# Gated attention and two mixture layers on one core: results of a unit stored one turn later, small units transposed in their first layer's arm, five banks for the first layer

## The chip, the cores and the metric

The program runs on one core of a Trainium2 chip. The metric is the device time of one execution in microseconds (us). The kernel before has a median of 763.64 us over three runs (763.48 to 764.53).

## What is computed

Three stages: a gated linear attention, a dense layer with the maximum of three products, and a mixture of eight experts in which each of 3072 tokens goes to the one expert with the largest logit. The change touches the third only.

```python
def _moe2_ref(x, w_gate, w_output_gate, w1, w2):
    ...
    e_idx = np.argmax(logits, axis=1)
    ...
    for e in range(E):                      # 8 experts
        mask = e_idx == e
        h = np.maximum(x[mask] @ w1[e], 0.0)          # 384 -> 1024
        ye = h @ w2[e]                                # 1024 -> 384
        out[mask] = gate_w[mask, None] * eom[mask, e, None] * ye
```

## The kernel before

**Units.** The tokens of each expert are cut into units of at most 256 tokens; the last unit of an expert may carry a tail of up to 64 more. Which unit belongs to which expert, and how full it is, is found on the chip, so the code of each unit has arms that registers choose (`by_kind`, L896 to L902, and `tc.If`). The kinds are 0 (256 tokens, two tiles of 128), 1 (64 or fewer, "alone"), 2 (256 and a tail of 64: three tiles) and 3 (128 or fewer: one tile). With these inputs fifteen units run. Units 0 and 1 are interleaved with the end of the dense layer. Units 2 to 14 have a turn each, `turn(u)` (from L1278), of kinds 0, 0, 2, **1**, 2, 0, 0, 0, 2, **1, 1**, 2, 3; turns 10 and later stand nested under a guard (L1298), and turns 15 to 19 are jumped over.

**A turn**, in program order on all engines: `load_meta(u+2)`; `gather(u+2)`, three indirect DMAs by POOL that fetch token rows `xg`; the low half of the split of w2 (cast on ACT L644, rest on DVE L645); `up(u)`, the first layer; the high half of the split; the weight DMA of s1 for u+2 by SP (L847); `tx(u+1)`, which transposes the next unit's rows into `cx` (L880, L887, L888) or, for kind 1, into `xF` (L891); `split1(u+1)`, the split of the next unit's w1 (six casts on ACT, six subtractions on DVE); `down(u)`, the second layer; and the weight DMA of s2. Each engine follows its own queue in this order and meets the others only through semaphores. PE's clock is granted in the profile's rows as a share of full speed.

**First layer** (`up_some`, L918): eight slices f of the hidden width, nine matmuls each, into one of three PSUM banks of pool psM in rotation. ACT (L919) and DVE (L922) take a bank away before PE may fill it again. For kind 1 (`alone` in `up`), the weights move and the 64 tokens stand still: twelve matmuls of 512 columns (L909) into one bank, copied by ACT as a whole into `hF` (L932).

**Second layer** (`down_tile`, L961 and L966): per tile 24 matmuls, then ACT scales by the gate into a tile `yo` (L973). For kind 1 (`alone` in `down`), PE first transposes `hF` (L985), ACT (L990) and DVE (L988) take the rectified halves, then sixteen matmuls of 384 columns follow (L909) and a sum of two halves (L948, L949, L950).

**Results.** `yo` comes from seven rotating tiles, and its scatter to `out` is issued by POOL inside the arm (`put`, L938), as soon as the tile is written. POOL therefore reads the kind and branches as PE, ACT and DVE do.

## Time and profile before

| | us |
|---|---|
| median of 3 runs | 763.64 |
| the profiled execution | 759.59 |
| its span, first to last instruction | 757.8 |
| PE busy | 705.9 (93%) |
| ACT busy / DVE busy / POOL busy | 288.5 / 397.7 / 126.8 |
| mean granted clock of TensorE | 0.978 |
| last matmul ends | 738.1 |

The profile counts an engine as busy while an instruction of it executes. Idle time of an engine is put down to the event that came last before it went on (its releaser). [...] The stretch that the change touches begins with the first layer of unit 0, at about 445 us.

### The profile page before, as it was taken

The page shows a single profiled execution, that of the slowest core. Times are in us where ns is not written, and L with a number is a line of the kernel's source. Part 1 is how long each engine was busy: PE and PEld are TensorE (multiplying, and loading weights), DVE is VectorE, ACT ScalarE, POOL GpSimd, SP SyncE. Part 2 cuts the span into 40 slices and gives each one's busy share as a digit, 9 for nine tenths or more (in the row PEclk, how much of TensorE's full clock was granted, in tenths as well). Part 3 has the DMA queues.
Part 4 walks back from the last instruction along what each step waited for, and adds up shares of the span by engine and source line. Part 5 has one row for each costly group of instructions (what it writes and reads, how often), then busy time and mean ns, then how long its engine had stood idle before and what let it go on. Part 6 is the DMA issues. An engine that isn't in the chain of part 4 may idle for free. (4 is left out here: it accounts for less than half of the span.)

```text
span 757.8 us, 14282 instructions
## 1 busy us (share of the span) xinstructions
PE 705.9 (93%) x5056; PEld 656.3 (87%) x5056; DVE 397.7 (52%) x929; ACT 288.5 (38%) x752; POOL 126.8 (17%) x136
## 2 busy tenths in 40 slices
PE   8999999999899999999999999999989999977980
PEld 8989999798799999999999999999949899954970
DVE  7968976477957547364143566532237422213640
ACT  4455344454444424335131243332236423224540
POOL 1000000011121202111111130422232322231220
PEclk9999999999999999999999999999989999997995
DMA  9823400651412215000000060214553113666310
GB/s 265 340 57 137 144 1 22 181 134 45 124 51 73 69 40 131 15 24 5 22 19 10 22 229 22 62 58 138 208 214 112 52 51 132 204 237 218 99 43 17
DMA packets 23407, 76.33 MB, mean 101 GB/s; under 512 B 8026, under 2 KB 12132, under 8 KB 20208
## 3 DMA queue, kind: packets, MB, share of 16 engines
q1 hardware_dynamic: 17424, 60.95, 24.6%
q0 software_dynamic: 4704, 12.91, 5.4%
q8 instruction: 67, 1.10, 0.6%
q10 hardware_dynamic: 1152, 0.89, 0.4%
q14 instruction: 60, 0.49, 0.2%
HBM read 89.26 MB, written 9.94 MB: 131 GB/s over the span
## 5 line engine op out<-in xcount | busy, mean ns | idle before, releaser
L918 PE MATMUL psM<-cx,w1H 128*128 128x256 f32 (+1 forms) x576 | 112.1, 292 | 5.3 <-DVE ch L922 4.9
L482 POOL TENSOR_TENSOR hL<-hm,hH 128x384 fp32r<-128x384 f32 x36 | 42.2, 1172 | 396.6 <-ACT hH L477 396.6
L456 PE MATMUL hps<-xH,wH 128*128 128x384 f32 x432 | 103.9, 347 | 1.4 <-ACT xH L367 1.3
L456 PE MATMUL hps<-xH,wL 128*128 128x384 f32 x432 | 98.4, 335 | 1.6 <-DVE wL L425 1.6
L918 PEld LDWEIGHTS psM<-cx,w1H 128*128 128x128 f32 x576 | 91.3, 188 | 8.8 <-DVE ch L922 4.3
L456 PE MATMUL hps<-xL,wH 128*128 128x384 f32 x432 | 98.6, 335 | 0.0
L961 PE MATMUL psP<-w2H,ch 128*128 128x384 f32 x368 | 96.8, 338 | 1.1 <-ACT w2H L644 1.1
L922 DVE SCALAR_TENSOR_TENSOR ch<-psM,ch 128x256 fp32r<-128x256 f32 (+1 forms) x128 | 43.9, 371 | 95.2 <-ACT ch L919 92.1
L918 PE MATMUL psM<-cx,w1L 128*128 128x256 f32 (+1 forms) x288 | 83.6, 290 | 0.0
L456 PEld LDWEIGHTS hps<-xH,wH 128*128 128x128 f32 x432 | 74.1, 188 | 7.4 <-ACT xH L367 2.1
L456 PEld LDWEIGHTS hps<-xH,wL 128*128 128x128 f32 x432 | 76.9, 188 | 2.3 <-DVE wL L425 2.3
L456 PEld LDWEIGHTS hps<-xL,wH 128*128 128x128 f32 x432 | 77.3, 188 | 0.2 <-DVE xL L368 0.2
L492 PE MATMUL ops<-wo,hH 128*128 128x400 f32 x258 | 68.5, 346 | 0.2
L961 PEld LDWEIGHTS psP<-w2H,ch 128*128 128x128 f32 x368 | 66.6, 188 | 2.0 <-issue 1.3
L463 DVE TENSOR_TENSOR hm<-hm,hps 128x384 f32<-128x384 f32 x48 | 26.4, 551 | 69.7 <-PE hps L456 62.7
L919 ACT ACTIVATE ch<-psM 128x256 fp32r<-128x256 f32 (+1 forms) x96 | 37.7, 402 | 64.8 <-PE psM L918 55.4
L938 POOL DMA_INDIRECT out<-yo,sidx x30 | 31.1, 1038 | 185.8 <-ACT yo L973 147.8
L961 PE MATMUL psP<-w2L,ch 128*128 128x384 f32 x184 | 61.5, 334 | 0.0
L857 POOL DMA_INDIRECT xg<-x2d,gidx x49 | 50.4, 1029 | 30.1 <-PE psM L918 12.2
L918 PEld LDWEIGHTS psM<-cx,w1L 128*128 128x128 f32 x288 | 54.2, 188 | 0.0
L477 ACT CAST hH<-hm 128x384 fp32r<-128x384 f32 x43 | 22.0, 513 | 81.0 <-DVE hm L466 77.2
L492 PEld LDWEIGHTS ops<-wo,hH 128*128 128x128 f32 x258 | 47.0, 188 | 1.3 <-ACT hH L477 0.5
(238 smaller groups left out, 1111.5 us busy)
## 6 DMA issues: line engine op xcount, KB each, us to landing
s1a<-in_ew SPq DMA_DIRECT2D x9, 1536.0 KB
s2a<-in_ew SPq DMA_DIRECT2D x9, 1536.0 KB
s1b<-in_ew SPq DMA_DIRECT2D x7, 1536.0 KB
s2b<-in_ew SPq DMA_DIRECT2D x7, 1536.0 KB
ws<-in_w SPq DMA_DIRECT2D x6, 1152.0 KB
at<-in_al SPq DMA_DIRECT2D x16, 336.9 KB
vt<-in_v SPq DMA_DIRECT2D x8, 576.0 KB
x2d<-xs SPq DMA_DIRECT2D x24, 192.0 KB
```

The costliest lines, as they stand in the source:

```text
L456: mm(ps, slab(a, f)[:, w, k], b[i][:, k], start=(n == 0), stop=(n == 8))
L463: nc.vector.tensor_max(m, m, ps)
L477: nc.scalar.copy(hH[i, f], m)
L482: (nc.gpsimd if not general and i > 1 else nc.vector).tensor_sub(hL[i, f], hps["m"], hH[i, f].bitcast(F32))
L492: mm(ps[:, :DM + NG], a[i, f][:, ts_], wo[f // 3][:, b, f % 3], start=(f + n == 0), stop=(f + n == 7))
L857: nc.gpsimd.indirect_dma_start(out=xg[u % 2, t][:p], out_offset=None, in_=x2d[:n, :], in_offset=bass.IndirectOffsetOnAxis(ap=gidx[:p, 3 * ...
L918: mm(ps, w[:, k, f * 128:(f + 1) * 128], x[:, k, :n], start=(k + m == 0), stop=(k + m == 4))
L919: nc.scalar.activation(chid(0, f, slice(0, n)), ps, AF.Relu)
L922: nc.vector.scalar_tensor_tensor(C["h"][f // 4][:, f % 4, to:to + b - a], ps[:, a:b], 0.0, chid(0, f, slice(a, b)).bitcast(F32), op0=ALU.m ...
L938: nc.gpsimd.indirect_dma_start(out=out[:, :], out_offset=bass.IndirectOffsetOnAxis(ap=sidx[:p, c:c + 1], axis=0), in_=y[:p], in_offset=Non ...
L961: mm(ps[:, :DM], chid(x, f, slice(128 * t, 128 * t + 128)), w[:, f], start=(f + n == 0), stop=(f == NE - 1 and n == 2))
```

## The change

1. **Results.** Three fixed tiles `C["y"]`, set to zero by POOL at the start, take the results of every unit. `put(u-1, ...)` stands in turn u behind `gather(u+2)`, outside all arms: three scatters each turn (two for the first units), whatever the kind; rows that carry no token have an index that the scatter leaves out. The last unit's three scatters come after all turns, with indices that DVE copied to `C["at"]`. POOL no longer reads the kind and has no arms.
2. **Small units.** In kind 1 the first layer goes in two halves of 256 columns (two banks, two copies), and the transposes of `hF` with their rectification move from `down`'s arm to the end of `up`'s arm, ahead of `tx(u+1)` and `split1(u+1)`.
3. **Banks.** In `up_some`, slices 3 and 4 use the two banks of pool psH: five banks in turn instead of three.
4. **Arms.** In `down`, tile 0 of kinds 0, 2 and 3 is one piece of code; the kind is asked after it.

```diff
@@ load_meta
-        kind[u] = nc.values_load(..., engines=(ET.PE, ET.Activation, ET.DVE, ET.Pool),
+        kind[u] = nc.values_load(..., engines=(ET.PE, ET.Activation, ET.DVE),
@@ hidden
+        C["y"] = [bp.tile([128, DM], F32, tag="hL", name="yo", bufs=7) for _ in range(3)]
+        for y in C["y"]:
+            nc.gpsimd.memset(y, 0.0)
@@ up_some
-            ps = bank(psM, "M", "psM1")[:, :n]
+            ps = (bank(C["psH"], "H", "psH") if f in (3, 4) else bank(psM, "M", "psM1"))[:, :n]
@@ up: alone
-            ps = bank(psM, "M", "psM1")
-            w = C["s1"][u % 2]
-            for k in range(3):
-                x = C["xF"][:, k * 128:k * 128 + 64]
-                halves(ps, 512, (x, x), [w[:, k, g * 512:(g + 1) * 512] for g in range(2)], k == 0, k == 2)
-            nc.scalar.copy(C["hF"][:, :512], ps)
+            w, h = C["s1"][u % 2], C["hF"]
+            for a in range(0, 512, 256):
+                ps = bank(psM, "M", "psM1")
+                for k in range(3):
+                    x = C["xF"][:, k * 128:k * 128 + 64]
+                    halves(ps, 256, (x, x), [w[:, k, g * 512 + a:g * 512 + a + 256] for g in range(2)], k == 0, k == 2)
+                nc.scalar.copy(h[:, a:a + 256], ps[:, :256])
+            for a in range(0, 512, 256):
+                ps = bank(C["psH"], "H", "psH")
+                for f in range(2):
+                    nc.tensor.transpose(ps[:, f * 128:(f + 1) * 128], h[:, a + f * 128:a + (f + 1) * 128], ident)
+                hs = h[:, 512 + a:768 + a]
+                if a:
+                    nc.vector.tensor_scalar_max(hs, ps[:, :256], 0.0)
+                else:
+                    nc.scalar.activation(hs, ps[:, :256], AF.Relu)
@@ put
+    def scatter(t, at):
+        p = WIDTH[t]
+        nc.gpsimd.indirect_dma_start(out=out[:, :], out_offset=bass.IndirectOffsetOnAxis(ap=at[:p], axis=0),
+                                     in_=C["y"][t][:p], in_offset=None, bounds_check=NTOK - 1, oob_is_err=False)
+    def put(u, tiles=3):
+        for t in range(tiles):
+            scatter(t, sidx[:, 3 * u + t:3 * u + t + 1])
@@ put_sum, down_tile
-        y, lo = out_tile(), bp.tile([128, DM], F32, tag="hm", name="ylo")
+        y, lo = C["y"][t], bp.tile([128, DM], F32, tag="hm", name="ylo")
...
-        put(u, t, y, 64)
...
+        nc.scalar.activation(C["y"][t], ps[:, :DM], AF.Copy, scale=gate[u % 2][:, t:t + 1])
@@ down
-            h = C["hF"]
-            for g in range(2):
-                p = bank(C["psH"], "H", "psH")
-                for f in range(2):
-                    fs = slice((2 * g + f) * 128, (2 * g + f + 1) * 128)
-                    nc.tensor.transpose(p[:, f * 128:(f + 1) * 128], h[:, fs], ident)
...
-        by_kind(u, {1: alone, 2: tiles(3), 3: tiles(1)}, tiles(2))
+        def whole():
+            down_tile(u, 0)
+            by_kind(u, {3: lambda: None, 2: lambda: [down_tile(u, t) for t in (1, 2)]}, lambda: down_tile(u, 1))
+        by_kind(u, {1: alone}, whole)
@@ turn
+        put(u - 1, 3 if u > NF else 2)
         fresh(u, split2, low)
         up(u)
+        if u >= NV - 1:
+            nc.vector.tensor_copy(C["at"], sidx[:, 3 * u:3 * u + 3])
...
+    for t in range(3):
+        scatter(t, C["at"][:, t:t + 1])
```

The order on ACT in turn 5, kernel before, from the next unit's branch on (L887 are the casts of `cx`, L644 the split of the next w1, L990 the rectification, L948 the result):

```order
L899 COMPARE_AND_BRANCH
L891 COPY xF<-psT 128x384
L899 UNCONDITIONAL_BRANCH
L887 CAST cx<-psT 128x3x128
L887 CAST cx<-psH 128x3x128
L887 CAST cx<-psH 128x3x64
L899 UNCONDITIONAL_BRANCH
L1272 COMPARE_AND_BRANCH
L644 CAST w1H<-s1a 128x512 x6
L1272 UNCONDITIONAL_BRANCH x2
L899 COMPARE_AND_BRANCH
L990 ACTIVATE hF<-psH 128x256
```

The same engine and turn in the changed kernel, the arm of kind 1 in the first layer:

```order
L936 COPY hF<-psM_7009 128x256
L936 COPY hF<-psM_7017 128x256
L945 ACTIVATE hF<-psH 128x256
L902 UNCONDITIONAL_BRANCH
L902 COMPARE_AND_BRANCH
```

and what now stands where the first piece stood:

```order
L890 CAST cx<-psT 128x3x128
L890 CAST cx<-psH 128x3x128
L890 CAST cx<-psH 128x3x64
L902 UNCONDITIONAL_BRANCH
L1273 COMPARE_AND_BRANCH
L644 CAST w1H<-s1a 128x512 x6
L1273 UNCONDITIONAL_BRANCH x2
L902 COMPARE_AND_BRANCH
L962 ACTIVATE yo<-psP,gate 64x384
```

The rectification moved from behind the six casts to ahead of the next unit's casts; the second layer's arm begins with the result.

ACT in the same turn, the first layer of 320 columns, before (a number behind psM is one filling of a bank):

```order
L919 ACTIVATE ch<-psM_7210 128x320
L919 ACTIVATE ch<-psM_7223 128x320
L919 ACTIVATE ch<-psM_7236 128x320
L919 ACTIVATE ch<-psM_7249 128x320
L919 ACTIVATE ch<-psM_7262 128x320
L919 ACTIVATE ch<-psM_7275 128x320
L919 ACTIVATE ch<-psM_7288 128x320
L919 ACTIVATE ch<-psM_7301 128x320
```

and in the changed kernel:

```order
L922 ACTIVATE ch<-psM_7034 128x320
L922 ACTIVATE ch<-psM_7047 128x320
L922 ACTIVATE ch<-psM_7060 128x320
L922 ACTIVATE ch<-psH 128x320 x2
L922 ACTIVATE ch<-psM_7099 128x320
L922 ACTIVATE ch<-psM_7112 128x320
L922 ACTIVATE ch<-psM_7125 128x320
```

The fourth and fifth slice went to psH; the first bank of psM is now filled again by the sixth slice and no longer by the fourth.

POOL in turn 3, before, behind its gathers (L857); the scatters stand in the arms (kinds 1, 2, 3 and 0, one behind the other):

```order
L899 COMPARE_AND_BRANCH
L938 DMA out<-yo,sidx 3072x384
L899 ISA
L899 UNCONDITIONAL_BRANCH
L899 COMPARE_AND_BRANCH
L938 DMA out<-yo,sidx 3072x384 x3
L899 UNCONDITIONAL_BRANCH
L899 COMPARE_AND_BRANCH
L938 DMA out<-yo,sidx 3072x384
L899 ISA x2
L899 UNCONDITIONAL_BRANCH
L938 DMA out<-yo,sidx 3072x384 x2
```

and the same turn in the changed kernel, gathers and scatters:

```order
L857 DMA xg_4714<-x2d,gidx 128x385
L857 DMA xg_4718<-x2d,gidx 128x385
L902 UNCONDITIONAL_BRANCH
L1273 UNCONDITIONAL_BRANCH
L902 UNCONDITIONAL_BRANCH
L857 DMA xg_5354<-x2d,gidx 64x385
L1273 UNCONDITIONAL_BRANCH
L951 DMA out<-yo,sidx 3072x384
L902 UNCONDITIONAL_BRANCH
L1273 UNCONDITIONAL_BRANCH
L951 DMA out<-yo,sidx 3072x384 x2
```

POOL's comparisons are gone from the turn; the three scatters of the unit before stand behind the gathers.

## Rows read from the trace of the kernel before

**Rows 1.** Page, part 1: busy us, share of the span, instructions.
```profile
PE 705.9 (93%) x5056; PEld 656.3 (87%) x5056; DVE 397.7 (52%) x929; ACT 288.5 (38%) x752; POOL 126.8 (17%) x136
```

**Rows 2.** Waits of PE, 440 to 745 us: total us, times, longest.
```profile
PE psM L918 <- DVE ch L922: 4.9, 5, 1.7
PE psM L909 <- issue: 4.5, 1, 4.5
PE psP L909 <- ACT hF L990: 4.3, 3, 2.2
PE psH L985 <- ACT w1H L644: 2.6, 2, 1.6
```

**Rows 3.** Timeline of turn 5: start, duration, engine, instruction [idle before <- releaser].
```profile
554.99 1.46 PE L909 MATMUL psM<-s1b,xF 128*64 128x512 f32 x6
...
557.28 0.93 POOL L938 DMA_INDIRECT out<-yo,sidx  x1 [4.38 <-DMA out<-yo,sidx]
...
558.45 3.23 ACT L644 CAST w1H<-s1a 128x512 fp32r<-128x512 f32 x6
...
559.17 0.67 PE L985 MATMUL psH<-ident,hF 128*128 128x128 f32 x4 [1.58 <-ACT w1H L644]
...
561.57 0.40 ACT L990 ACTIVATE hF<-psH 128x256 f32<-128x256 f32 x1
...
562.02 0.91 PE L909 MATMUL psP<-s2b,hF 128*64 128x384 f32 x2 [2.17 <-ACT hF L990]
```

**Rows 4.** Stretches: length, busy of PE, PEld, DVE, ACT, POOL, clock, DMA.
```profile
560.50:567.50 7.00, 5.48 (x17) 1.88 (x17) 2.74 (x5) 1.49 (x5) 2.32 (x2) 0.52 0.58 229
693.00:698.00 5.00, 4.69 (x17) 1.68 (x17) 1.52 (x3) 0.26 (x1) 0.00 (x0) 0.58 0.04 12
699.00:738.00 39.00, 35.63 (x236) 33.95 (x235) 21.33 (x54) 19.56 (x46) 10.20 (x10) 1.00 0.28 82
```

**Rows 5.** Timeline of PE in turns 11 and 12.
```profile
675.84 2.80 PE L909 MATMUL psP<-s2b,hF 128*64 128x384 f32 x16 [0.34 <-ACT hF L990]
...
683.14 4.49 PE L909 MATMUL psM<-s1a,xF 128*64 128x512 f32 x12 [4.50 <-issue]
...
688.23 0.52 PE L880 MATMUL psT<-ident,xg 128*128 128x128 f32 x3 [0.59 <-PE psM L909]
...
690.46 1.08 PE L985 MATMUL psH<-ident,hF 128*128 128x128 f32 x4 [1.06 <-ACT w1H L644]
...
693.31 0.91 PE L909 MATMUL psP<-s2a,hF 128*64 128x384 f32 x2 [1.76 <-ACT hF L990]
```

**Rows 6.** Line L899, 672 to 760 us: duration ns, least, median, most; PE's sequencer.
```profile
L899 PEldq COMPARE_BRANCH  x22: 63/215/5753, 672.7 to 735.5; - x22
```

**Rows 7.** Page, part 3: packets, MB, share of sixteen DMA engines.
```profile
q8 instruction: 67, 1.10, 0.6%
```

**Rows 8.** Timeline of turn 7, first layer.
```profile
592.98 1.76 ACT L644 CAST w2H<-s2b 128x384 fp32r<-128x384 f32 x4 [0.37 <-ACT ylo L949]
...
593.00 0.28 PE L918 MATMUL psM<-cx,w1L 128*128 128x256 f32 x1
...
594.06 0.28 PE L918 MATMUL psM<-cx,w1L 128*128 128x256 f32 x1
...
596.42 0.51 PE L918 MATMUL psM<-cx,w1H 128*128 128x256 f32 x2 [1.73 <-DVE ch L922]
```

**Rows 9.** Line L1350, the program's end, 672 to 758 us: duration ns.
```profile
L1350 POOLq DRAIN  x3: 46/111/6605, 750.3 to 757.5; - x3
```

**Rows 10.** Line L1298, the guard, 670 to 758 us: duration ns, first and last start.
```profile
L1298 ACTq EVENT_SEMAPHORE  x2: 17/17/17, 741.9 to 741.9; - x2
L1298 POOLq INC_SWDGE_SEM  x1: 1753/1753/1753, 747.9 to 747.9; - x1
```

**Rows 11.** Timeline of the end.
```profile
739.07 1.03 POOL L938 DMA_INDIRECT out<-yo,sidx  x1 [9.91 <-ACT yo L973]
```

**Rows 12.** DMA issues, 700 to 758 us: count, us from issue to landing.
```profile
out<-yo,sidx POOLq DMA_INDIRECT x5, 2.9
```

## The prediction

> **What bounds the kernel now.** I read the page first, then the waits of PE, then the timeline around each, last the granted clock of those stretches and the program's end. The page shows PE at 93% of the span and no other engine above 52% [rows 1]: only what shortens PE's work, its waits, or what lies behind its last matmul can count. The waits of PE in the stretch that the change touches are in four rows of size [rows 2]: 4.9 us, in five pieces, for a bank of the first layer that DVE empties; 4.5 us in one piece put down to "issue", so to nothing that the profile shows; 4.3 us for ACT's rectification of `hF`; 2.6 us for the split of w1. The last two belong to the three small units (turns 5, 11, 12). Their timeline shows why. In turn 5 PE can transpose `hF` only at 559.17, and ACT rectifies at 561.57, because the six casts of the next unit's w1 (3.23 us from 558.45) stand ahead in its queue; PE waits 1.58 and 2.17 us [rows 3]. Then the clock is at half: from 560.5 to 567.5 it was granted 0.52 on average, and PE's 17 matmuls there took 5.48 us [rows 4], where the sixteen of the same shape in turn 11 took 2.80 [rows 5]. What PE did before the fall was to sit idle.

> **The change part by part.** All terms are against the profiled execution.

> *Turn 5.* Before, 1.58 + 2.17 = 3.75 us of waiting [rows 3]. After, the transposes follow the first layer directly and ACT's queue holds only copies and the rectification ahead of the casts. What is new: the second half's transposes wait for its copy, which I price at 0.6, a little above the 0.40 of the rectification of as many columns [rows 3] for the way there and back. The clock: 5.48 − 2.80 = 2.7 if PE no longer idles [rows 4, 5]; I take 2.6, and give back 0.75 for the first matmuls at half clock. PE's sequencer leaves the arm by a branch; such branches took 0.2 us as a median and up to 5.75 [rows 6]. They sit where PE's code is fetched: the instruction queue moved 1.10 MB in 67 packets, 16 KB each [rows 7], so a branch into a block not yet there waits for one. The new code leaves the arm with less work queued on PE, and I price the part not hidden at 1.0. Sum −3.75 + 0.6 − 2.6 + 0.75 + 1.0 = **−4.0** (−5.5 when the branch is hidden, −1 when it takes 4).

> *Turns 11 and 12.* Both are small. In turn 11 the wait ahead of the second layer is short already, 0.34 [rows 5]: −0.3. In turn 12 there are 0.59, 1.06 and 1.76 us [rows 5]; of 3.4 I keep 0.6 as above: −2.8. The second layer of turn 12 ran at a clock of 0.58 and took 4.69 [rows 4] against 2.80: −1.9. The transposes took 1.08 against 0.67 in turn 5 [rows 3, 5]: −0.4. The 4.50 "issue" ahead of turn 12's first layer [rows 5] I leave as it is: the longest branch of L899, 5.75 us [rows 6], is PE's way from the end of turn 11 into turn 12, and the change keeps a jump into the next block there. So the first layer of turn 12, 4.49 us after that pause, also keeps its half clock. Exits of two arms, less hidden than now: +0.4. Sum −0.3 − 2.8 − 1.9 − 0.4 + 0.4 = **−5.0** (−8 if the 4.5 pause goes for the most part; −2 if the exits cost 3 more).

> *Five banks.* The longest of the five waits shows the pattern: ACT splits w2 for 1.76 us from 592.98, the three banks fill, and PE waits 1.73 until DVE has emptied one [rows 8]. One bank lasts PE 1.06 us (593.00 to 594.06, nine matmuls [rows 8]), so two more cover 2.1, more than the longest wait. psH is free then: its last readers are the casts of `cx` a turn earlier. Of 4.9 us [rows 2] I take **−4.3** and keep 0.6 for units of 320 columns, whose banks are emptied more slowly (−4.9 to −1; −1 if ACT, late once, stays late over all eight slices).

> *Smaller matmuls.* Twelve of 512 columns become 24 of 256 in each small unit. The nearest rows, both at full clock: six of 512 in 1.46 us [rows 3], sixteen of 384 in 2.80 [rows 5], so 0.48 and 0.46 ns a column; the size carries almost no price. Three times 0.13: **+0.4** (0 to +1.2, the end for weight loads that no longer hide).

> *Results one turn later.* In the middle of the kernel this costs nothing so long as the three scatters of unit u−1 have landed before ACT writes unit u's result, a first layer and more later. From 700 us on a scatter lands 2.9 us after its issue [rows 12]; three in a row make 8.7, and each waits for the one before. A turn takes some 10. POOL has that time: it is 17% busy [rows 1], and its gathers stand ahead of the scatters as now. SP's weight DMAs are in no queue of POOL's. The three tiles are also released by this: ACT's wait would be for a scatter of the turn before.

> *The end.* Before: POOL issues the last scatter at 739.07 [rows 11]; then the engines jump past the turns that don't run: ACT meets the others at 741.9, POOL only then goes on, to 1.75 us of its own count from 747.9 [rows 10], then a drain of 6.6 us from 750.3 [rows 9]; the span ends at 757.8. After: POOL jumps early, since nothing of the last turn holds it back, and the last three scatters wait for ACT to have joined, at 741.9: issued at 742.0, 744.9 and 747.8, the last for 1.0 us, then a branch and the drain from 749.3 rather than 750.3: **−1.0**. Bounds: −4 if three land in 2 us each or the drain shrinks, +3 if the drain counts from the last landing.

> Sum: −4.0 − 5.0 − 4.3 + 0.4 − 1.0 = −13.9. The span goes from 757.8 to 743.9, and the profiled execution from 759.59 to 745.7. The median of the runs lies 763.64 − 759.59 = 4.05 above the profiled one, which I take to stay: **749.7**.

> **The rivals.**

> *The exits eat the gain.* The end of the first layer's arm now comes right behind the transposes. If each branch there stalls PE as the longest did (5.75 [rows 6]), turns 5, 11 and 12 get nothing: the clock falls in the pause as it did. There remain −4.3 + 0.4 − 1.0 = −4.9: 758.7. For it: the 4.5 pause shows that such a stall exists. Against it: the median branch takes 0.2 us, and ACT, DVE and PE's own queue have some 1 us of work at that point. [...]

> *Serial scatters on three tiles*, the case on the other side. In turn 5, while DMA was full, a scatter's successor waited 4.38 us for it [rows 3], so one takes about 5.4 from issue to issue. If that is the rule, the last three end 3 × 5.4 − 3 × 2.9 = 7.5 later, and ACT waits for tile 0 in the turns behind small units, three times about 3 us: −13.9 + 7.5 + 9 = +2.6 on top, and PE, which waits for ACT in turn, loses about 1 more: 763.64 + 3.6 = 767.2. It decides from about 5 us a scatter. Against it: DMA's share is 0.28 from 699 to 738 [rows 4], where the scatters took 2.9. [...]

> *It doesn't do what it says.* If the next unit's rows or weights come no sooner than PE needs them, the waits of turns 5, 11 and 12 change their names only, and psH, in use by `tx` and `alone`, hands back what five banks gave: 763.2.

> **How the numbers follow.** Forecast 0.72, exits 0.15, serial scatters 0.08, no effect 0.05. The bounds of the terms add up to −22.4 and +0.2 if all end on one side; not all will. I put 742.5 as the low end (half of that way below) and the high end at 758.7, so that the second case lies inside; what is left out is 0.13 of rivals and some 0.05 of the forecast. Within 0.2% is ±1.5 us, about what a measurement of this kernel can tell from no change. Faster: the forecast and most of the second case, 0.86; same 0.06; slower 0.08.

> **What would show it.** In the profile after: in turn 5 PE waits no more than 1 us around L940 and L909 and the granted clock stays at 1.00 from 560 to 567; the waits of PE for a bank of the first layer in units of 256 columns are gone; the pause between turns 11 and 12 still stands; the last scatters are issued from about 742 less the gain, each some 3 us behind the one before. I am wrong if long branches stand at the end of the first layer's arm in turns 5 and 12, if ACT waits for a scatter ahead of L985 or L962, or if the time from PE's last matmul to the end is more than 22 us where it was 757.8 − 738.1 = 19.7.

## The result

The changed kernel took 771.07 us (median of four runs, 770.31 to 775.29) against 763.62 before: a ratio of 1.0106, 95% interval 1.0068 to 1.0144. It is slower by about 8 us, where 14 us less were forecast; the time lies above the range. The profiled execution took 770.53 us with a span of 768.8 (757.8 before).

PE's row of the page, to be laid beside [rows 1]: more busy time, at a smaller share.

```profile
PE 709.4 (92%) x5092; PEld 663.6 (86%) x5092; DVE 396.9 (52%) x935; ACT 289.1 (38%) x755; POOL 145.2 (19%) x152
```

The waits of PE in the changed kernel from 430 us on (total us, times, longest), against [rows 2]:

```profile
PE psT L883 <- issue: 6.5, 2, 6.0
PE psM L912 <- issue: 3.4, 1, 3.4
PE psM L921 <- ACT ylo L963: 3.2, 1, 3.2
PE psM L921 <- issue: 3.1, 1, 3.1
PE psP L974 <- issue: 2.2, 7, 0.7
```

Of the four rows of before three are gone, as forecast: no wait for a bank of the first layer, none for the rectification of `hF`, none for the casts of w1. What stands there instead is three long pauses put down to "issue", one wait of 3.2 us behind a copy of ACT, and small ones in every turn.

Where the 11.0 us of span came from, by the starts of the same matmuls in the two traces (the profiled execution of the kernel before was 4.1 us faster than its median, that of the changed kernel 0.5 us, so the 11.0 us are more than the 8.1 of the ratio). Unit 2's first layer starts at 494.67 before and at 494.99 after, and the stretches behind that are these:

| stretch | before, us | after, us | change |
|---|---|---|---|
| start to unit 2's first layer | 494.67 | 494.99 | +0.3 |
| turns 2 to 4 (to unit 5's first layer) | 58.98 | 61.71 | +2.7 |
| turn 5 (to unit 6's first layer) | 13.69 | 15.12 | +1.4 |
| turns 6 to 10 | 103.03 | 104.95 | +1.9 |
| turns 11 and 12 | 27.60 | 24.73 | −2.9 |
| turns 13 and 14, to PE's last matmul | 40.15 | 44.40 | +4.3 |
| from there to the end | 19.6 | 22.9 | +3.3 |

In the stretch from 0 to 440 us, which the kernels share, profiled executions of them differ by a few us (436 to 440 us at the same matmul), and this wandering belongs to no part of the change. (Of the +0.3 in the first row +1.4 come before 437 us and −1.1 behind, where units 0 and 1 have the five banks already.) So below totals are compared by their ratio to the kernel before on the same chip, and profiles by stretches behind unit 2. "Scaled" is the ratio less 1, times 763.6.

Three readings of the changed kernel's trace lead to the experiments.

**The next unit's transposes wait in every turn.** Timeline of turn 7 (start, duration, engine, instruction [idle before <- releaser]):

```profile
604.29 0.49 PE L883 MATMUL psT<-ident,xg 128*128 128x128 f32 x3
604.54 0.38 ACT L922 ACTIVATE ch<-psM 128x256 fp32r<-128x256 f32 x1 [0.70 <-PE psM L921]
604.98 0.88 PE L883 MATMUL psH<-ident,xg 128*128 128x128 f32 x6 [0.20 <-ACT ch L922]
606.14 0.44 PE L974 MATMUL psP<-w2H,ch 128*128 128x384 f32 x1 [0.28 <-issue]
```

The transposes into psH start only when ACT has emptied the last bank of the first layer (604.54 + 0.38), though that bank is one of psM. In the kernel before, the same place, they start while ACT still empties that bank:

```profile
601.86 0.49 PE L880 MATMUL psT<-ident,xg 128*128 128x128 f32 x3
602.11 0.38 ACT L919 ACTIVATE ch<-psM 128x256 fp32r<-128x256 f32 x1 [0.68 <-PE psM L918]
602.19 0.82 PE L880 MATMUL psH<-ident,xg 128*128 128x128 f32 x6
602.93 0.44 PE L961 MATMUL psP<-w2H,ch 128*128 128x384 f32 x1
```

From the first transpose to the second layer it takes 1.85 us; before it took 1.07. Over the nine turns whose unit is not small and has a successor the sum is 18.0 us against 9.7.

**ACT waits for scatters behind the small units.** Timeline from turn 11 to unit 13's first layer:

```profile
679.54 1.04 POOL L951 DMA_INDIRECT out<-yo,sidx  x1 [10.28 <-ACT hF L936]
...
688.62 0.57 ACT L962 ACTIVATE yo<-psP,gate 64x384 f32<-64x384 f32 x1 [6.80 <-DMA out<-yo,sidx]
...
701.91 1.04 POOL L951 DMA_INDIRECT out<-yo,sidx  x1 [3.16 <-DMA out<-yo,sidx]
...
707.54 0.58 ACT L962 ACTIVATE yo<-psP,gate 64x384 f32<-64x384 f32 x1 [8.46 <-DMA out<-yo,sidx]
...
708.67 0.90 PE L921 MATMUL psM<-cx,w1H 128*128 128x320 f32 x2 [3.17 <-ACT ylo L963]
```

Unit 10's tile 0 is scattered at 679.54; the scatter has not let go of the tile when unit 11's result is ready, and ACT stands until 688.62. One turn later the same: a scatter of 701.91 holds ACT until 707.54, ACT empties no bank of unit 13's first layer meanwhile, and PE stands for 3.17 us. In the kernel before ACT waited for no scatter.

**The end.** POOL's last three scatters, and (second fence) the drain behind them (durations in ns, first and last start):

```profile
751.36 0.98 POOL L951 DMA_INDIRECT out<-yo,at  x1 [8.77 <-ACTq L1302]
757.04 0.98 POOL L951 DMA_INDIRECT out<-yo,at  x1 [4.69 <-DMA out<-yo,at]
759.46 0.92 POOL L951 DMA_INDIRECT out<-yo,at  x1 [1.44 <-DMA out<-yo,at]
```

```profile
L1358 POOLq DRAIN  x3: 44/113/8227, 759.8 to 768.5; - x3
```

The first does wait for ACT to have joined, as forecast, but they are 5.7 and 2.4 us apart, and the drain takes 8.2 us where it took 6.6 [rows 9].

### The profile page after: what moved, and what is told of

The parts are those of the page before. It is cut to its first block, busy times and chain, and to the rows that moved or that the text cites. A ratio compares the mean times of both kernels' runs of the same rounds, so it can differ in the third digit from the quotient of the medians.

```text
span 768.8 us, 14271 instructions
## 1 busy us (share of the span) xinstructions
PE 709.4 (92%) x5092; PEld 663.6 (86%) x5092; DVE 396.9 (52%) x935; ACT 289.1 (38%) x755; POOL 145.2 (19%) x152
## 5 line engine op out<-in xcount | busy, mean ns | idle before, releaser
L921 PE MATMUL psM<-cx,w1H 128*128 128x256 f32 (+1 forms) x432 | 86.4, 297 | 6.3 <-ACT ylo L963 3.2
L921 PEld LDWEIGHTS psM<-cx,w1H 128*128 128x128 f32 x432 | 70.6, 194 | 8.0 <-issue 3.7
L925 DVE SCALAR_TENSOR_TENSOR ch<-psM,ch 128x256 fp32r<-128x256 f32 x96 | 32.4, 369 | 80.1 <-ACT ch L922 76.0
L951 POOL DMA_INDIRECT out<-yo,sidx x40 | 40.4, 1009 | 147.3 <-ACT yo L985 37.1
L857 POOL DMA_INDIRECT xg<-x2d,gidx x49 | 55.4, 1131 | 49.3 <-DVE cx L891 23.4
L921 PE MATMUL psM<-cx,w1L 128*128 128x256 f32 (+1 forms) x216 | 64.0, 296 | 0.0
L492 PE MATMUL ops<-wo,hL 128*128 128x400 f32 x129 | 44.5, 345 | 0.5 <-POOL hL L482 0.5
L922 ACT ACTIVATE ch<-psM 128x256 fp32r<-128x256 f32 (+1 forms) x72 | 27.7, 401 | 41.9 <-PE psM L921 31.1
```

What stands on the lines that cost most here:

```text
L492: mm(ps[:, :DM + NG], a[i, f][:, ts_], wo[f // 3][:, b, f % 3], start=(f + n == 0), stop=(f + n == 7))
L857: nc.gpsimd.indirect_dma_start(out=xg[u % 2, t][:p], out_offset=None, in_=x2d[:n, :], in_offset=bass.IndirectOffsetOnAxis(ap=gidx[:p, 3 * ...
L921: mm(ps, w[:, k, f * 128:(f + 1) * 128], x[:, k, :n], start=(k + m == 0), stop=(k + m == 4))
L922: nc.scalar.activation(chid(0, f, slice(0, n)), ps, AF.Relu)
L925: nc.vector.scalar_tensor_tensor(C["h"][f // 4][:, f % 4, to:to + b - a], ps[:, a:b], 0.0, chid(0, f, slice(a, b)).bitcast(F32), op0=ALU.m ...
L951: nc.gpsimd.indirect_dma_start(out=out[:, :], out_offset=bass.IndirectOffsetOnAxis(ap=at[:p], axis=0), in_=C["y"][t][:p], in_offset=None, ...
```

## The experiments

| kernel | ratio to before (95%) | scaled, us against before |
|---|---|---|
| changed kernel | 1.0106 (1.0068 to 1.0144) | +8.1 |
| 1 before, five banks | 0.9918 (0.9874 to 0.9962) | −6.3 |
| 2 before, arm | 1.0255 (1.0185 to 1.0325) | +19.5 |
| 3 before, results and second layer | 1.0148 (1.0091 to 1.0204) | +11.3 |
| 4 before, arm and banks | 1.0177 (1.0124 to 1.0231) | +13.5 |
| 5 changed, arm in psM | 0.9973 (0.9954 to 0.9993) | −2.1 |
| 6 changed, two sets of tiles | 1.0060 (1.0037 to 1.0084) | +4.6 |
| 7 changed, code 92 instructions on | 1.0106 (1.0074 to 1.0139) | +8.1 |
| 8 changed, code 184 on | 1.0144 (1.0117 to 1.0170) | +11.0 |
| 9 changed, two scatters less at the end | 1.0040 (1.0017 to 1.0063) | +3.1 |
| 10 as 5, results as before | 0.9836 (0.9804 to 0.9867) | −12.5 |
| 11 before, banks, arm in psM | 1.0044 (1.0021 to 1.0067) | +3.4 |
| 12 as 5, two sets of tiles | 0.9975 (0.9950 to 1.0001) | −1.9 |
| 13 as 10, arm undone | 0.9794 (0.9764 to 0.9823) | −15.7 |
| 14 as 10, three banks | 0.9929 (0.9901 to 0.9958) | −5.4 |

### One part at a time

**1. Five banks alone.**

```diff
-            ps = bank(psM, "M", "psM1")[:, :n]
+            ps = (bank(C["psH"], "H", "psH") if f in (3, 4) else bank(psM, "M", "psM1"))[:, :n]
```

> The kernel before with the five banks alone. Theory 1 (the banks cost more than they give): the five waits of PE for a first-layer bank, 4.9 us, go, but in each of the nine turns whose successor is not small PE stands in tx until ACT has emptied the last bank of the first layer, some 0.9 us from tx's start to the second layer's start as in the changed kernel (1.07 before, 1.7 to 2.4 after), so +8: about 767 us. Rival (that delay comes from the rearranged second layer or the scatters): -4.9, about 759 us, tx to second layer 1.1 us as before.

Measured 757.21 us, ratio 0.9918. My theory fell: with psH in the first layer the transposes of the next unit start as early as before, and 1.1 us later the second layer. The five waits for a bank of [rows 2] are gone and nothing has come in their place. What it kept is the pause into unit 12 (5.7 us here, 4.5 before); waits of PE from 494 us on:

```profile
PE psM L909 <- issue: 5.7, 1, 5.7
PE psP L909 <- ACT hF L990: 4.7, 3, 2.2
```

**2. The arm alone** (the two halves and the transposes, as in the change).

> The kernel before with the small units' transposes in the first layer's arm alone. [...] About 759 us; 764 if the exits stall as in the changed kernel. Rival (the arm itself is slower, whatever the exits): 766 or more.

784.16 us, ratio 1.0255: the arm costs 20 us by itself. It is here, without any bank of psH in `up_some`, that tx waits in every turn: 22.0 us in the nine turns, 9.7 before. Waits of PE from 494 us on, two rows of several:

```profile
PE psM L918 <- issue: 10.9, 4, 8.3
...
PE psP L971 <- issue: 6.8, 8, 1.8
```

The second row is the second layer's start, eight times: PE has run dry in tx, and the comparisons of the kind that follow, 0.2 us each as a median [rows 6], lie bare. The first row is pauses of the sequencer, the longest 8.3 us, into unit 13. The gain was there where it was sought (the second layers of turns 5 and 12 took 2.80 us, 5.4 and 4.7 before), but the rival, which said 766 or more, has the sign, at many times its least size.

**3. The results and the rearranged second layer alone.**

> The kernel before with the results one turn later and the rearranged second layer alone (three banks, transposes in the second layer). Theory: ACT waits 6 to 8 us for the scatter of tile 0 in the turns behind small units (11, 12) and the end is 3 us longer: about 770 us. Rival (the waits of ACT are harmless, because the small units were bound by code and clock already): 764 to 766, all of it at the end.

774.94 us, ratio 1.0148; the theory's mechanism holds, its size does not: +11.3 us where 6 were expected, and ACT's longest wait is 14.3 us where 6 to 8 were. The two fences are ACT's and PE's longest wait around turns 11 to 13:

```profile
ACT yo L952 <- DMA out<-yo,sidx: 20.6, 2, 14.3
```

```profile
PE psM L921 <- ACT ylo L953: 7.9, 1, 7.9
```

The pause of 4.5 us into unit 12 is not in this kernel: unit 12's first layer follows at once (run 13 comes back to that). So the results alone may cost more here than the 11.3 us, by what the rearranged second layer gives.

**4. Arm and banks, results as before.**

> The changed kernel without the later results: arm and banks on the kernel before. If the three parts add up: +4 of the banks and -4 of the arm: about 764 us, and no wait of ACT for a scatter. If the results' waits were covered by others: 770 as the changed kernel.

777.13 us, ratio 1.0177, slower than the changed kernel by the ratios, though the intervals touch. The parts add up (−6.3 + 19.5 = +13.2, measured +13.5), but not as expected, since neither part was what I took it for. That the results, +11 on the kernel before, go along with 5 us less on this one suggests that their edit brings something too: the rearranged second layer, which has fewer comparisons ahead of its first matmul (run 13 isolates it).

### The wait in tx

**5. The arm's transposes in banks of psM.**

```diff
-                ps = bank(C["psH"], "H", "psH")
+                ps = bank(psM, "M", "psM1")
                 for f in range(2):
                     nc.tensor.transpose(ps[:, f * 128:(f + 1) * 128], h[:, a + f * 128:a + (f + 1) * 128], ident)
```

> The changed kernel with the arm's four transposes in banks of psM, as before the first layer's, and not in psH. Theory: psH, written in an arm, makes tx of every turn wait for ACT to have emptied the whole first layer; without that tx takes 1.14 us again (1.56 to 1.75 now) and the second layer follows 1.1 us after tx's start (1.7 to 2.5 now), in nine turns together -7 us: 764 us. Rival (tx waits because of the five banks in psH, or for its rows): no change, 771 us.

761.45 us, ratio 0.9973: 10 us less than the changed kernel, by the bank alone. Turn 7 again:

```profile
600.49 0.49 PE L883 MATMUL psT<-ident,xg 128*128 128x128 f32 x3
...
600.74 0.38 ACT L922 ACTIVATE ch<-psM 128x256 fp32r<-128x256 f32 x1 [0.69 <-PE psM L921]
600.82 0.82 PE L883 MATMUL psH<-ident,xg 128*128 128x128 f32 x6
...
601.57 0.44 PE L974 MATMUL psP<-w2H,ch 128*128 128x384 f32 x1
```

The transposes into psH start while ACT still has its last bank to empty, and the second layer follows 1.08 us after the first transpose. Over the nine turns it is 10.3 us again (18.0 in the changed kernel): −7.7. The rest is the pause in turn 5, 3.3 us here and 6.0 there. So the wait comes with psH in the arm of kind 1, in turns that skip this arm too. `up_some` fills psH in both other arms, and tx does not wait for that (run 1: 9.9 us in nine turns). Why the one arm makes the next user of the bank wait until the arms are over, and the other two do not, is not shown; the runs show the bank: with psH in that arm tx waits (runs 2, 4 and the changed kernel), with psM it does not (runs 5, 10, 11, 12 and 14).

### The results one turn later

**6. Two sets of tiles**, for even and odd units (`C["y"][u % 2 * 3 + t]`).

> The changed kernel with two sets of three result tiles, for even and odd units (the last three scatters take the even set, which is right for these fifteen units only). Theory: ACT no longer waits for the scatter of tile 0 (6.8 us in turn 11, 8.5 us in turn 12), PE's wait of 3.2 us in unit 13's first layer and the half clock there go: -5 us, 766 us, with the end as long as in the changed kernel (22.9 us). Rival (the first layer of unit 13 is slow for its code, and ACT's wait lies beside that): within 1.5 us of 771.

768.40 us, ratio 1.0060: −3.5 us, a little less than expected. ACT's row "<- DMA out" is gone from its waits, and so is PE's 3.2 us inside unit 13's first layer, which takes 13.6 us instead of 17.4. The pauses are as in the changed kernel; the one into unit 13 (3.4 us) is now put down to ACT's copy L963, not to "issue". The end takes 23.8 us.

**9. Without the last two scatters** (the last unit has one tile).

```diff
-    for t in range(3):
+    for t in range(1):
         scatter(t, C["at"][:, t:t + 1])
```

> The changed kernel without its last two scatters (tiles 1 and 2 of the last unit, which carry no token here). Theory: from PE's last matmul to the end it took 22.9 us with three scatters in a row, the later two issued 5.7 and 8.1 us after the first; without them the drain begins some 5 us sooner: end 18 to 19 us, 766 us. Rival (the drain, 8.2 us instead of 6.6, is what grew, and the branch of POOL past the general program is as long as the two scatters): end 21 us or more, 769 or more.

763.73 us beside 761.08 of the kernel before, ratio 1.0040. From PE's last matmul to the end it is now 14.6 us, 8.3 less than in the changed kernel and 5 less than before. The scatter and (second fence) the drain:

```profile
752.88 0.98 POOL L951 DMA_INDIRECT out<-yo,at  x1 [8.49 <-ACTq L1302]
```

```profile
L1358 POOLq DRAIN  x3: 44/113/8133, 753.2 to 761.9; - x3
```

The drain still takes 8.1 us but begins right behind the one scatter. The gain of 5.0 us by the ratios is what was expected; the end is shorter than either side had it. The two scatters are on the path in full, 759.8 − 753.2 with PE's end 1.6 us later here. With one scatter the end would have gained 5 us; with three in a row it lost 3.3. Some 2 us of that gain belong to the rearranged second layer: with it and the results as before the end took 17.4 to 18.0 us (runs 10, 13, 14), without it 19.2 to 20.3 (the kernel before, runs 1, 2, 4, 11).

**10. The results as before** (rotating tiles, scatters in the arms), on the kernel of run 5. PE's code is the same as there, instruction by instruction.

> The changed kernel with the arm's transposes in psM (761.5 us) and the results as before: rotating tiles, scatters in the arms. PE's code lies as in that kernel. Theory: what the later results cost is ACT's wait for a scatter (2.6 us of PE's waiting in unit 13, and its clock) and 3.3 us at the end: -6 to -7 us, 755 us, with the pauses at the branches (3.3 into unit 6, 3.3 into unit 12, 3.1 into unit 13) as there. Rival (POOL's arms and their comparisons cost as much): 760 to 762.

748.64 us, ratio 0.9836: 10.5 us less than run 5 by the ratios, more than I expected. By the traces: unit 13's first layer 12.6 us instead of 16.8, the end 18.0 instead of 23.2, and 0.1 us in each first layer. POOL's comparisons, which the change removed, took 0.04 us each as a median (0.03 to 0.06 from 660 to 695 us in this kernel) and cost nothing that shows. PE's waits from 494 us on, the first three rows (the first is the pauses into units 6 and 13, 2.7 and 3.6 us, behind branches of 4.3 and 4.9; run 5 has them as "issue", 3.3 and 3.1):

```profile
PE psM L918 <- ACT w2H L644: 6.3, 2, 3.6
PE psM L909 <- issue: 3.2, 1, 3.2
PE psT L880 <- issue: 1.2, 3, 0.6
```

**12. Both: arm in psM and two sets of tiles.**

> The changed kernel with the arm's transposes in psM and two sets of result tiles (the last scatters take the even set, right for these inputs). Theory: -2.7 us as the second set gave alone: 758.5 us, no wait of ACT for a scatter, and the end as long as ever (23 us). Rival (the gain of both is the same time): 761.

758.73 us, ratio 0.9975, the same as run 5 within the intervals. ACT's wait is gone and the end is still 23.4 us. By the traces it gained 2.8 us (240.0 to 237.2 from unit 2's first layer to PE's last matmul); the ratios do not show it, so whether the two gains add is open. So ACT's wait is 0 to 3 of the 10.5 us between runs 5 and 10; the end is 5.2 of them, and for the rest no run shows the cause.

### The pauses

**7 and 8. PE's code shifted**, by 46 transposes (92 in the second kernel) in an arm that is never run:

```diff
             for a in range(0, 512, 256):
                 ps = bank(psM, "M", "psM1")
+                if u == NF and not a:
+                    for _ in range(46):
+                        nc.tensor.transpose(ps[:, :128], ident, ident)
```

In the changed kernel PE pauses for 6.0 us in turn 5, for 3.4 into unit 12 and for 3.1 into unit 13. The theory of both runs is that these pauses go with the place of PE's code. In the first, those in turn 5 and into unit 13 were to go and the one into unit 12 was to stay. The rival is that PE waits there for rows or weights. Which of the pauses would go was worked out from where blocks of PE's code begin, and that no trace or run shows; what can be read is whether they move.

> The changed kernel with 46 transposes added to an arm that is not run (kind 1 of unit 2), so that all later code of PE lies 92 instructions further on. [...] With the clock of unit 5's second layer -8 us: 763. Rival (PE waits there for rows or weights): all three pauses stay, 771.

> The same with 92 transposes, 184 instructions. Theory: the pause of 6.0 us in turn 5 goes, the one into unit 12 (3.4 us) goes, since its branch stays in one block; the one into unit 13 (3.1) stays: -8 to -10 us, 762. Rival: as in the run before, no difference, 771.

771.33 us (1.0106) and 775.75 (1.0144). Of the times both expectations were wrong; of the places they were right in the first and half right in the second. Waits of PE from 494 us on, in the first:

```profile
PE psT L883 <- issue: 5.6, 1, 5.6
PE psM L912 <- issue: 3.5, 1, 3.5
PE psM L921 <- issue: 2.7, 1, 2.7
```

and in the second:

```profile
PE psT L883 <- issue: 6.1, 1, 6.1
PE psH L883 <- issue: 4.7, 2, 4.5
PE psH L943 <- ACT hF L939: 3.8, 3, 3.5
```

In the first the pause of turn 5 has moved from the first layer's exit to the second layer's (2.7 us, into unit 6), the one into unit 13 has gone, the one into unit 12 has stayed, and a new one of 5.6 stands behind unit 12's first layer, one transpose into tx. In the second the pause in turn 5 is 4.5 us, eight transposes into tx, the one into unit 12 has gone, the one into unit 13, which was to stay, has gone too (1.4 us, put down to ACT), and one of 6.1 stands behind unit 11's first layer, two transposes into tx. (The third row of the second fence is PE waiting for ACT's copy in unit 12's arm; ACT stood there for an event that the profile calls "remote", and what it was is not known.) The same instructions for the same data, only at other addresses: so the pauses go with the place of PE's code, not with rows or weights. A pause of 1.6 to 1.8 us at turn 2, in both, is the jump over the filler itself.

The DMA records of the traces show what moves while PE waits. The instruction queue moves blocks of 16 KB (67 packets, 1.10 MB [rows 7]). From unit 2 to PE's last matmul the sixteen kernels have 37 branches of PE longer than 4 us (4.3 to 6.6); in each of them such a block begins to move after the branch has begun, and the branch ends 1.3 to 1.5 us after the block has landed. The changed kernel's longest, from 560.04 to 566.42, has its block from 564.12 to 565.08. The pauses of 5.6, 4.5 and 6.1 us in the middle of tx end 1.3 to 1.6 us behind such a block too. I read this as PE standing for code that is not there yet. Most blocks are not waited for in this way: 29 to 37 of them come in that stretch of a kernel, and one to four of its branches are so long.

### What the arm and the second layer are worth

**11. Banks and arm in psM on the kernel before**, so with its second layer.

> The kernel before with five banks (757.2 us alone) and the arm's transposes in psM. Theory: the arm alone, taken out of psH, gives the clock of units 5 and 12 back and its waits (3.3 and 3.3 us), less the pauses for code that then show: 753 to 757. If the transposes in an arm cost PE the wait in tx in whatever bank: 777, as with psH.

763.74 us, ratio 1.0044: neither, and 9.6 us more than the banks alone (run 1). The wait in tx is gone (1.1 us as before), so it was the bank; but PE stands 2.4, 4.5 and 5.8 us for "issue" and the like in turns 11 and 12.

**13. The kernel of run 10 with the transposes back in the second layer**: five banks and the rearranged second layer, and nothing else of the change.

```diff
         def alone():
+            h = C["hF"]
+            for g in range(2):
+                p = bank(C["psH"], "H", "psH")
...
         def whole():
             down_tile(u, 0)
             by_kind(u, {3: lambda: None, 2: lambda: [down_tile(u, t) for t in (1, 2)]}, lambda: down_tile(u, 1))
```

> The kernel of 748.6 us (five banks, second layer rearranged, results as before, arm's transposes in psM) with the small units' transposes back in the second layer. If the arm out of psH is worth its term: the waits for the rectification (2.2, 0.3 and 1.8 us) and for the casts (1.6, 1.1) come back with the half clock: 755 to 758. Rival (the rearranged second layer gave the time, the arm nothing, since the pauses for code take it): 748 to 750.

745.84 us, ratio 0.9794, the fastest of all. The rival holds: the arm, in psM, is worth nothing or less (0.9836 with it, so 3 us more, but the intervals overlap; the traces have 2.6 us more from unit 2 to PE's end), and the rearranged second layer is worth about 9.5 us (0.9918 to 0.9794, give or take 4). By the traces these are 5.5 us in turns 11 and 12, 1.4 in turns 13 and 14 and 2.3 at the end. Its waits from 494 us on:

```profile
PE psP L909 <- ACT hF L990: 4.4, 3, 2.2
PE psT L880 <- DVE gate L877: 1.7, 1, 1.7
PE psH L880 <- DMA xg<-x2d,gidx: 1.4, 2, 0.7
PE psH L985 <- ACT w1H L644: 1.1, 1, 1.1
```

The waits that the arm was to remove are still there, in part under other names. What is gone is the pause into unit 12. Its timeline in turns 11 and 12:

```profile
672.82 1.78 PE L909 MATMUL psP<-s2b,hF 128*64 128x384 f32 x10
674.43 2.75 PE L909 MATMUL psM<-s1a,xF 128*64 128x512 f32 x12
678.92 0.52 PE L880 MATMUL psT<-ident,xg 128*128 128x128 f32 x3 [1.75 <-DVE gate L877]
680.14 0.52 PE L880 MATMUL psH<-ident,xg 128*128 128x128 f32 x3 [0.70 <-DMA xg<-x2d,gidx]
```

and with five banks alone (run 1), the same place:

```profile
681.62 4.67 PE L909 MATMUL psM<-s1a,xF 128*64 128x512 f32 x12 [5.66 <-issue]
```

Unit 12's first layer follows unit 11's second layer at once and at the full clock, 2.75 us instead of 5.66 + 4.67. The longest branch of L899 still takes 5.0 us there (673.62 to 678.63), now with that first layer queued on PE ahead of it, so that of the 1.75 us behind it the branch ends last, as late as the row that the profile names; behind that the next unit's gathered rows are what is late (0.70 us and more). In run 3, the other kernel with the rearranged second layer and the transposes in it, unit 12's first layer follows at once too. The code that PE and the others run has become shorter. The instruction queue from 494 us to PE's last matmul (packets, MB, share), run 1 and, second, run 13:

```profile
q8 instruction: 36, 0.59, 1.1%
```

```profile
q8 instruction: 29, 0.48, 0.9%
```

Seven blocks of 36 are gone, as between the kernel before (36) and run 3 (29), and of PE's branches over 4 us one is left, where the kernel before has two and the kernels with the arm and this second layer (the changed kernel, runs 5, 10, 12 and 14) have three. Whether fewer blocks or another place of their edges gave the time, the runs don't separate.

**14. The kernel of run 10 with three banks.**

> The kernel of 748.6 us with three banks in the first layer. If the banks' term stands by itself: the waits of PE for a bank come back (4.9 us in five pieces in the kernel before): 753 to 754. Rival (the waits were those of a late ACT behind small units and the arm covers them): 749 to 750.

756.89 us, ratio 0.9929 against 0.9836: five banks are worth 7 us here (give or take 3), where the first side expected the 4.9 of their waits: unit 13's first layer alone took 16.6 us, 12.6 in run 10 (run 14's profiled execution is the slowest of its ten).

## Why the prediction was wrong, step by step

**What bounds the kernel** was read rightly in part. The fastest kernel (run 13) is without the waits for a bank and the pause into unit 12, both in [rows 2]; the other two rows, for which the arm was built, are still in it. The signs of being wrong that the prediction named came: a long branch behind the arm in turn 5, ACT waiting for a scatter ahead of L962, and 22.9 us at the end.

**The frame of the sum.** The 4.05 us between the profiled execution and the median, taken to stay, were 0.5 in the changed kernel. The low end of the range, 742.5, is not half of the way down to the sum of the low bounds (745.5 would be), and −5.5 for turn 5 with a hidden branch is −5.0 by its own terms; neither changes anything, as the time lies above the range. That a scatter at the end lands in 2 us, as the low bound of that term (−4) has it, no run shows; in the changed kernel the three were issued 5.7 and 2.4 us apart.

**Five banks** (−4.3): sign and mechanism right, the size too small; alone −6.3, beside the other parts −7.1.

**Turn 5** (−4.0, measured +1.4 in the changed kernel). The rectification moved ahead, the 3.75 us of waiting went, and the second layer took 3.43 us instead of 5.39; the step that failed is the price of 1.0 for the branch at the arm's exit, which cost 6.0. PE's branches of L902 from 556 to 575 us:

```profile
L902 PEldq COMPARE_BRANCH  x6: 68/224/6382, 560.0 to 570.7; - x6
```

The longest took 6.4 us and PE stood for 6.0 of it. I had the row that spoke for this, 5.75 us [rows 6], gave it to the rival as a whole ("the exits eat the gain", 0.15) and took 1.0, near the median of 0.2, for the forecast. That such a branch waits for a block of code I had put down beside [rows 7], and the runs bear it out in the small units: pauses moved with the code's place in runs 7 and 8, and a block of 16 KB lands 1.3 to 1.5 us before each long branch ends. Pauses of the same size also came behind the arm's exit and not at it: those of 4.5 to 6.1 us in the middle of tx in runs 7 and 8, one to eight transposes on. The clock fell in the pause (to 0.50 at 562.95), and the stretch behind it had 0.70 as a mean:

```profile
566.40:572.00 5.60, 5.52 (x26) 2.95 (x27) 3.94 (x8) 4.39 (x9) 1.00 (x1) 0.70 0.20 74
702.00:719.00 17.00, 13.83 (x74) 13.38 (x72) 6.19 (x19) 5.80 (x14) 7.10 (x7) 0.70 0.33 111
```

(Columns as in [rows 4]; the second row is unit 13's first layer.)

**Turns 11 and 12** (−5.0, measured −2.9): the three waits went, unit 12's second layer ran at the full clock (2.80 us, 4.69 before), and the pause into unit 12 stayed, as forecast (3.4 instead of 4.5). But the same kind of pause came up into unit 13 (3.1 us), which I had priced with 0.4.

**The arm in every turn** was not priced at all: the term stood at nothing. The step that moved the transposes was costed for the three units that use the arm, not for those that jump over it. Run 5 gives it: about 10 us, of which 7.7 in tx. With that taken away, the arm is still worth nothing (run 10 against run 13) or costs 9.6 us (run 11 against run 1, with the second layer as before), where −9.0 was forecast: what it takes from the waits for `hF` it gives to pauses for code, three branches over 4 us in run 10 for one in run 13.

**Results one turn later** ("in the middle of the kernel this costs nothing", and −1.0 at the end). Run 10 against run 5: 10.5 us. Two mistakes of sizing with the right rows at hand, of which the end is shown as a cost (5.2 us), and ACT's wait only in the traces (2.8 us, run 12). The 2.9 us of [rows 12] came from the quiet stretch behind 700 us; [rows 3] had a scatter's successor waiting 4.38 us in a turn in which weights move, with the DMA engines busy for 0.70 of the time (552.9 to 557.3) where it was 0.27 from 700 to 738. In the changed kernel the scatter of 679.54 held its tile for 9 us, at a DMA share of 0.98. And I said that the tiles are free a turn later without counting that a small unit's turn is some 12 us long and its scatters stand behind gathers and each other. That rival ("serial scatters on three tiles", 0.08) had mechanism and place right, down to the three tiles and the end; that its 767 us lies near the 771 is luck, since it kept the −9.0 of the arm, which did not come, and had nothing for tx. At the end the three scatters were 5.7 and 2.4 us apart, not 2.9, and the drain was 1.6 us longer; why the drain is longer is not shown.

**The smaller matmuls** (+0.4): 24 of 256 columns took 2.81 us and twelve of 512 2.79 to 2.80, so +0.0.

**The rearranged second layer** was named in the change and given no price. It is worth about 9.5 us with five banks (run 13 against run 1), the largest single gain in the change, and 16 beside the arm (run 10 against run 11).

So the sum was wrong in three places that all point the same way, some 10 us each: the wait in tx (not seen), the results (sized at −1.0), the arm's own gain (sized at −9.0, worth 0). Two gains, the banks and the second layer, together −15.7 with nothing else of the change, were hidden beneath them. By runs that differ in one part each, the way from the kernel before to the changed one is −6.3 (banks, run 1), −9.4 (second layer, run 13), +3.2 (arm in psM, run 10), +10.4 (results, run 5) and +10.2 (psH in the arm), each give or take 3 to 4: +8.1. In another order the parts have other sizes (runs 3, 4, 11 and 14), so these are not prices that add in any kernel. What stays open: why psH in one arm makes tx wait while psH in the two others does not, what of the second layer's gain is fewer blocks and what their place, a part of what the results cost, and the drain.

## What to carry to other kernels

When work moves into a conditional arm, price it in the iterations that skip the arm too. Here the nine turns that skip it took 18.0 us from the first transpose of tx to the second layer with psH in the arm and 10.3 with psM; a trial with another bank told them apart. A wait that goes from a path on which an engine's code is jumping is not a gain until the branch behind it is shown to be hidden; take the longest such branch of the trace (5.75 us here), not the median (0.2). Chained transfers that each wait for the one before should be priced with the landing time of the busiest stretch in which they can stand (a tile was held for 9 us, where 2.9 were taken); at this program's end they lay on the path in full, 5.0 us for two scatters.
